# Taking the attention loop of a fused attention and two-layer kernel three steps at a time

## The chip, the cores and the metric

The kernel runs on one NeuronCore of a Trainium2 chip. The metric is device time of one execution in microseconds (us), lower is better. The kernel before took 828.43 us, the median of three runs (824.09 to 830.15). The profiled execution, from which every row below comes, took 831.28 us.

Engines: PE is TensorE (matrix products), DVE is VectorE, ACT is ScalarE, POOL is GpSimd, SP issues the DMAs. Each works through its own list of instructions in the order in which the program was written; semaphores hold an instruction back until what it needs is there.

## The reference, cut to what matters

```python
# q, k, v: 2 batches, 8 heads, 768 tokens, 64 wide; 16 cluster centroids a head
q_assign = argmax(q_n @ c_n.T);  k_assign = argmax(k_n @ c_n.T)
scores = where(q_assign == k_assign, (q @ k.T) / 8, -1e9)
scores = scores - max(scores, axis=-1)
attn = exp(scores);  attn = attn / (sum(attn, axis=-1) + 1e-9)
x = attn @ v                                  # then 1536 tokens x 512
x = f(x @ w_in) @ w_out                       # 512 -> 2048 -> 512; f(h) = h if h >= 1, 0 if h <= -1, else (h + 1)**2 / 4
x = rmsnorm(x);  out = (silu(x @ w_gate) * (x @ w_val)) @ w_out2
```

## The kernel before, in words

Attention goes over 8 **pairs** of heads (`NP`), and a pair over 12 **steps**: two halves of the queries (384 each) by six tiles of 128 keys. The global step number is `g`; pair p scores at g = 12p to 12p + 11. The program is written out by hand, without a scheduler, so what stands first in the code stands first on its engine.

For one step of a pair the kernel does the following.

- **Scores** (`score`, L348): for each of two heads two products of 128 x 384 on PE into one of three banks of PSUM (`st`), and an exponential on ACT (L357) into a tile P of 14. POOL adds the P tiles up (L363, L367), ten additions a half.
- **Values** (`values`, L369): P times v for both heads, each into one half of PE's columns (128 x 64 products). The two heads are side by side, and each product is recorded as two instructions.
- **Maxima** (`maxq`, L300): the row maxima, for the pair that scores later. Two products `mp` on PE into two banks (`mx`, two buffers), and a reduction of each on DVE (L319). A product needs the bank that the reduction two before it has read. After six steps of maxima, a small reduction (L322), a transposition on PE (`mt_ps`, L339), a copy on ACT (`mt`, L343) and a DMA bring the maxima into a row of A, where the scores' second product (L355) reads them.
- **Finish** (`finish`, L397), some steps after each half: piece 0 (ACT: logarithm, exponential, `r`), 1 and 2 (DVE: `e`, L413 and L416), 3 (DVE: `x`, L419), 4 (ACT: `xh`), 5 (DVE: `xl`, L423). The sums of P that it needs come from PE (`sums`, L391).
- **Preparation** (`prep`, L143) of a pair, about two pairs ahead: load q and k, split each into a high part (ACT) and a low part (DVE, L157), similarities with the centroids (PE, `simt`), a copy (ACT), transposition (PE, `sim`), the one-hot cluster (DVE: `mx` L187, `eq` L192, `e` L195, `m` L198, `oh` L202), transposition (PE, `oht_ps`), and the placing of the parts into A and B by DMA on SP's queue.

`attention_steps(g, n)` writes n steps: the maxima's copy of the previous group, the copy of finished values, then for each step its maxima, scores and other engines' work, then conversion of weights (`follow`, from g = 76), then the values of the **two steps before** (g - 2 and g - 1), sums, transpositions and similarities. From g = 0 on the kernel before calls it with n = 2. The small banks (`misc`, two buffers) serve the sums, the similarities and all transpositions by turns.

From g = 76 DVE and ACT also convert weights for the layers behind (`conv`, six DVE operations a slice, `conv(2)` a group and `conv(4)` from g = 84), and `TAIL` puts the first products of the layers between the last groups. The layers then run on PE without a pause to the end; the change does not touch them.

Of the kernel before, what the change touches and what calls it, by code (L numbers as in the profile page):

```python
# [12 lines left out]
ALU = mybir.AluOpType  # L13
# [23 lines left out]
def clustered_attention_two_ffn(  # L37
# [105 lines left out]
    def prep(p, o, on_tensor):  # L143
# [89 lines left out]
        def place(kind, s=slice(0, 2)):  # L233
# [19 lines left out]
            8: [lambda: sims_copy(), lambda: place("kh")],  # L253
            9: [lambda: place("qh")],
            10: [lambda: first_max()],
            11: [lambda: is_max(0), lambda: place("kl", 0)],
            12: [lambda: is_max(1), lambda: first_rank(), lambda: place("kl", 1)],
            13: [lambda: one_hot(), lambda: place("ql", 0)],
            14: [lambda: place("ql", 1)],
            17: [lambda: turn_out()],  # L260
# [32 lines left out]
        if p == 2:  # L293
            del todo[0]
            todo[-4] = [lambda: load_qk(p)]
        for f in (tensor if on_tensor else todo).get(o, ()):
            f()


    def maxq(p, j):  # L300
# [3 lines left out]
        if j == 0:  # L304
            st["M2", p] = ap.tile([128, 12, 2], F32, tag="M2", bufs=2, name=f"M2{p}")
            st["M", p] = ap.tile([128, 12], F32, tag="M", bufs=2, name=f"M{p}")
        if p == 0 and j < 8 and j % 3:

            mp = ps0.tile([128, 2, 512], F32, tag=f"mx{j % 3}", name=f"mp{p}_{j}")
            mp = [mp[:, 0], mp[:, 1]]  # L310
        else:
            mp = [ps.tile([128, 512], F32, tag="mx", bufs=2, name=f"mp{p}_{j}_{n}") for n in range(2)]
        for n in range(2):
            nc.tensor.matmul(mp[n][:, 0:HALF], A[0:112, h, 0, 128 * qt:128 * qt + 128],  # L314
                             Bk[0:112, h, 0, HALF * n:HALF * n + HALF], start=True, stop=True)
        if p == 0 and j < 10:
            warm(3 if j < 9 else 24, mp[1][:, HALF:512])
        for n in range(2):
# [490 lines left out]
    def preps(g, on_tensor=False):  # L809
        for p in range(NP):  # L810
            prep(p, g - PREP0[p], on_tensor)
# [186 lines left out]
```

## Time and profile before

| | before |
|---|---|
| median of three runs | 828.43 us |
| profiled execution | 831.28 us, of which the span from first to last instruction 829.5 us |
| PE busy | 806.4 us (97%) |
| DVE busy | 607.2 us (73%) |
| ACT busy | 350.2 us (42%) |
| POOL busy | 155.7 us (19%) |
| mean granted clock of TensorE | 0.985 |

Shares over the whole span say little here: attention takes roughly the first 260 us, and the layers the rest. Within attention there is a start of about 62 us, then pairs 1 to 5 (those that score at g = 12 to 71) at one even pace, then the seventh and eighth pair, where weights are converted as well. A busy PE is not a PE at its peak: an instruction that starts late because the array changes its layout looks busy all the same. So the start times of neighbouring PE instructions are read, not their busy time.

### The profile page before, as it was taken

Reading aid. Unit: us, or ns where it says so; the run is one execution under the profiler, and the core shown is the slowest. Engines: PE = TensorE matmul, PEld = TensorE weight load, DVE = VectorE, ACT = ScalarE, POOL = GpSimd, SP = SyncE. Lnnn points to the kernel's source line nnn. Section 1 sums busy time; section 2 is a strip of 40 time slices with the busy share of each in tenths; the row PEclk is TensorE's granted clock in tenths of the full one; section 3 lists DMA queues with packets and bytes.
Section 4 is the critical chain, followed back from the end, with each engine's and each line's share of the span. In section 5 each row is a group of like instructions: output and inputs, shape, how many; then the busy total and the mean of one; then the engine's idle time right before and its main releaser. Section 6 shows DMA issues by size and latency. Waiting matters only on the chain.

```text
span 829.5 us, 10698 instructions
## 1 busy us (share of the span) xinstructions
PE 806.4 (97%) x3817; PEld 611.7 (74%) x3817; DVE 607.2 (73%) x1101; ACT 350.2 (42%) x662; POOL 155.7 (19%) x163
## 2 busy tenths in 40 slices
PE   7789999999899999999999999999999999999998
PEld 3556665666455788888888888888888888888887
DVE  7658899988855788788777878898887875633333
ACT  5446666665435655553444353533333222211110
POOL 0368888888500000000000000000000000000000
PEclk9989999999899999999999999999999999999999
DMA  8956555653232537644443443145665343000003
GB/s 202 202 141 163 136 134 137 147 136 131 70 102 80 187 120 220 195 151 139 141 152 117 154 136 102 57 127 171 203 203 178 126 153 102 0 1 1 1 25 127
DMA packets 33336, 105.15 MB, mean 127 GB/s; under 512 B 5098, under 2 KB 5444, under 8 KB 33284
## 3 DMA queue, kind: packets, MB, share of 16 engines
q1 hardware_dynamic: 33284, 104.48, 42.5%
q8 instruction: 30, 0.49, 0.3%
q14 instruction: 22, 0.18, 0.1%
HBM read 81.02 MB, written 3.15 MB: 101 GB/s over the span
## 4 chain that ended last, share of the span: by engine, by line
PE 88%; DVE 8%; DMA 1%; ACT 1%; issue 0%; POOL 0%; ACTq 0%; POOLq 0%; DVEq 0%
PE h L545 40%; PE y L594 9%; PE y L593 9%; PE y L595 9%; PE pv L375 6%; PE mp L314 4%; DVE M L319 3%; PE sc L355 3%; PE sc L354 3%; PE sum L394 1%; DVE e L416 1%; PE sum L383 1%; DMA kraw<-kT 1%; PE simt L165 1%; DMA aa<-mt 1%; PE xt L663 1%
## 5 line engine op out<-in xcount | busy, mean ns | idle before, releaser
L367 POOL TENSOR_TENSOR acc<-acc,P 128x384 f32<-128x384 f32 x112 | 124.3, 1141 | 17.0 <-ACT P L357 17.0
L319 DVE TENSOR_REDUCE M<-mp 128x1 f32<-128x384 f32 x192 | 97.3, 549 | 35.1 <-PE mp L314 33.6
L357 ACT ACTIVATE P<-sc 128x384 f32<-128x384 f32 x192 | 84.5, 490 | 77.1 <-PE sc L355 68.2
L545 PE MATMUL h<-xh,bb 128*128 128x512 f32 x360 | 115.5, 390 | 0.0
L545 PE MATMUL h<-xh,aa 128*128 128x512 f32 x336 | 108.6, 391 | 0.0
L496 ACT ACTIVATE raw<-raw 128x512 f32<-128x512 f32 x60 | 40.7, 679 | 111.5 <-DVE bits L494 97.6
L545 PE MATMUL h<-xh,place 128*128 128x512 f32 x264 | 85.8, 392 | 0.0
L610 DVE TENSOR_TENSOR Y<-y,Y 128x512 f32<-128x512 f32 (+1 forms) x85 | 57.8, 681 | 31.9 <-PE y L595 31.8
L375 PE MATMUL pv<-P,v 128*64 128x384 f32 x384 | 80.2, 524 | 0.0
L545 PEld LDWEIGHTS h<-xh,bb 128*128 128x128 f32 x360 | 67.6, 188 | 14.7 <-issue 0.6
L545 PEld LDWEIGHTS h<-xh,aa 128*128 128x128 f32 x336 | 63.1, 188 | 15.0 <-issue 1.8
L355 PE MATMUL sc<-aa,bb 97*128 97x384 f32 x192 | 66.7, 348 | 3.6 <-DMA aa<-mt 3.6
L545 PE MATMUL h<-xl,bb 128*128 128x512 f32 x180 | 70.1, 390 | 0.0
L354 PE MATMUL sc<-aa,bb 112*128 112x384 f32 x192 | 67.0, 349 | 1.5 <-ACT P L357 1.5
L545 PE MATMUL h<-xl,aa 128*128 128x512 f32 x168 | 65.5, 390 | 0.0
L314 PE MATMUL mp<-bb,aa 112*128 112x384 f32 x192 | 59.7, 387 | 4.7 <-DVE M L319 4.6
L565 DVE SCALAR_TENSOR_TENSOR a<-h,a 128x512 f32<-128x512 f32 x48 | 33.1, 691 | 38.7 <-ACT a L561 38.7
L545 PEld LDWEIGHTS h<-xh,place 128*128 128x128 f32 x264 | 49.6, 188 | 11.1
L314 PEld LDWEIGHTS mp<-bb,aa 112*128 112x128 f32 x192 | 33.6, 196 | 30.7 <-DVE M L319 13.1
L545 PE MATMUL h<-xl,place 128*128 128x512 f32 x132 | 52.0, 394 | 0.0
L494 DVE SCALAR_TENSOR_TENSOR bits<-raw,bits 128x512 uint32<-128x512 uint32 x68 | 48.3, 711 | 1.5
L375 PEld LDWEIGHTS pv<-P,v 128*64 128x64 f32 x384 | 24.3, 142 | 31.4 <-issue 27.7
(188 smaller groups left out, 1546.5 us busy)
## 6 DMA issues: line engine op xcount, KB each, us to landing
raw<-w_out SPq DMA_DIRECT2D x28, 512.0 KB
mid<-w_out SPq DMA_DIRECT2D x28, 511.8 KB
raw<-w_in SPq DMA_DIRECT2D x16, 512.0 KB
mid<-w_in SPq DMA_DIRECT2D x16, 511.8 KB
raw<-w_gate SPq DMA_DIRECT2D x12, 512.0 KB
raw<-w_val SPq DMA_DIRECT2D x12, 512.0 KB
mid<-w_gate SPq DMA_DIRECT2D x12, 511.8 KB
mid<-w_val SPq DMA_DIRECT2D x12, 511.8 KB
```

The lines of the kernel that those rows point to most:

```text
L314: nc.tensor.matmul(mp[n][:, 0:HALF], A[0:112, h, 0, 128 * qt:128 * qt + 128], Bk[0:112, h, 0, HALF * n:HALF * n + HALF], start=True, stop= ...
L319: nc.vector.tensor_reduce(st["M2", p][:, j, n:n + 1], mp[n][:, 0:HALF], axis=AX.X, op=ALU.max)
L354: nc.tensor.matmul(sc, Bk[0:112, h, 0, ks], A[0:112, h, 0, qs], start=True, stop=False)
L355: nc.tensor.matmul(sc, Bk[0:97, h, 1, ks], A[0:97, h, 1, qs], start=False, stop=True)
L357: nc.scalar.activation(P, sc, AF.Exp, scale=0.125)
L367: nc.gpsimd.tensor_tensor(acc, acc, P, op=ALU.add)
L375: nc.tensor.matmul(pv[64 * h:64 * h + 64, 0:HALF], st["v", p][:, h, kt], st["P", p, i, h], start=(kt == 0), stop=(kt == NT - 1))
L545: nc.tensor.matmul(h, w[:, wi, fs], x[:, kc, cs], start=(n == 0), stop=(n == 11))
L593: nc.tensor.matmul(y[:, c], g[:, 0, fs], w[:, 0, c], start=(m == m0), stop=False)
L594: nc.tensor.matmul(y[:, c], g[:, 0, fs], w[:, 1, c], start=False, stop=False)
L595: nc.tensor.matmul(y[:, c], g[:, 1, fs], w[:, 0, c], start=False, stop=(m == ms[-1]))
L610: nc.vector.tensor_tensor(Y[:, c], y[:, c], Y[:, c], op=ALU.add)
```

## The change

From g = 12 to g = 83 (`TWOS = 84`), which are the second to the seventh pair, the loop takes three steps at a time instead of two. Within such a group PE's list goes one `mp`, one head's two score products, one `mp`, and so on, where before two `mp` stood together; all work of the other engines for the three steps comes after the scores of the group; and the values of **the same** three steps follow, where before they were those of the two steps before. At g = 10 the two-step loop takes two steps' values more, and the group at g = 84 therefore has none. The maxima run two `mp` products further ahead from g = 12.

The preparation is laid out for three-step groups: the split of k and q, the similarities and so on are moved by one to three steps, the copy of the similarities (`sims_copy`) to the start of a group, and one of the two placings `kl` ahead of the maxima's DMA on SP's queue. Finish pieces come one to three steps later. v is loaded three steps earlier. Conversion begins at g = 75 with `conv(3)` a group. The group that completes six maxima now always issues their transposition itself, which at the start puts the first pair's `mt_ps` ahead of the `mp` of its step 6.

```diff
-        for i, (nm, piece) in enumerate((("k", 0), ("k", 1), ("q", 0), ("q", 1))):
-            todo.setdefault(i + (3 if p > 2 else 7), []).insert(0, lambda nm=nm, piece=piece: split(nm, piece))
-        tensor = {7: [lambda: sims()], 9: [lambda: sims_back()], 15: [lambda: turn()]}
...
+            3: [lambda: split("k", 0)],
+            4: [lambda: split("k", 1), lambda: split("q", 0)],
+            6: [lambda: place("kh"), lambda: split("q", 1)],
+            7: [lambda: place("qh")],
+            8: [lambda: place("kl", 0)],
+            9: [lambda: first_max(), lambda: is_max(0), lambda: place("kl", 1)],
+            10: [lambda: is_max(1), lambda: place("ql", 0)],
+            11: [lambda: place("ql", 1)],
+            12: [lambda: first_rank(), lambda: one_hot()],
+            15: [lambda: turn_out()],
+        }
+        tensor = {5: [lambda: sims()], 6: [lambda: sims_back()], 12: [lambda: turn()]}
...
-        for piece, ds in enumerate(((7, 3), (8, 4), (9, 4), (10, 5), (11, 5), (12, 6))):
+        for piece, ds in enumerate(((7, 7, 3), (8, 9, 4), (9, 10, 4), (10, 11, 5), (11, 13, 5), (12, 15, 6))):
...
+        if n == 3:
+            for k in range(g, g + n):
+                preps(k, 2)
+        due = max(0, 2 * (max_to + 1 - MAX0) - at["max"])
         for k in range(g, g + n):
+            if n == 3:
+
+                for h in range(2):
+                    i = 2 * (k - g) + h
+                    maxima(due * (i + 1) // 6 - due * i // 6)
+                    scores_of(k, h)
+                continue
...
+        if n == 3:
+            for k in range(g, g + n):
+                other_engines(k)
         then()
+        while at["value"] <= min(to, END - 1):
+            vp, vi = divmod(at["value"], 12)
...
+            values(vp, vi)
...
-        conv(2 if g < 84 else 4)
+        conv(3 if g < 84 else 4)
...
-    for g in range(0, END + 6, 2):
+    steps = [(g, 2, g - 1 + 2 * (g == 10), g + 1) for g in range(0, 12, 2)]
+    steps += [(g, 3, g + 2, g + 3) for g in range(12, TWOS, 3)]
+    steps += [(g, 2, g - 1, g + 1) for g in range(TWOS, END + 6, 2)]
+    for g, n, to, max_to in steps:
...
-        if g == 74:
+        if g == 75:
             free += places[0:6]
```

PE's list before, at the end of the two-step group in which the third pair scores its steps 0 and 1. `mp` are the maxima of the same pair, `sc_1_0` the scores of step 1 and head 0, `P_10_0` those of step 10 of the pair before:

```order
L354 MATMUL sc_1_0_1090<-aa_109,bb_110 128x384
L355 MATMUL sc_1_0_1090<-aa_109,bb_110 128x384
L314 MATMUL mp_9_0_1097<-bb_110,aa_109 128x384
L314 MATMUL mp_9_1_1098<-bb_110,aa_109 128x384
L354 MATMUL sc_1_1_1103<-aa_109,bb_110 128x384
L355 MATMUL sc_1_1_1103<-aa_109,bb_110 128x384
L375 MATMUL pv_1_996<-P_10_0_1023,v_690 64x384
L375 MATMUL pv_1_996<-P_10_1_1029,v_690 64x384
L375 MATMUL pv_1_996<-P_11_0_1039,v_690 64x384
L375 MATMUL pv_1_996<-P_11_1_1051,v_690 64x384
```

PE's list of the change, at the end of the three-step group in which the same pair scores its steps 0 to 2:

```order
L328 MATMUL mp_11_0_1124<-bb_110,aa_109 128x384
L368 MATMUL sc_2_0_1127<-aa_109,bb_110 128x384
L369 MATMUL sc_2_0_1127<-aa_109,bb_110 128x384
L328 MATMUL mp_11_1_1133<-bb_110,aa_109 128x384
L368 MATMUL sc_2_1_1137<-aa_109,bb_110 128x384
L369 MATMUL sc_2_1_1137<-aa_109,bb_110 128x384
L387 MATMUL pv_0_1085<-P_0_0_1094,v_977 64x384
L387 MATMUL pv_0_1085<-P_0_1_1102,v_977 64x384
L387 MATMUL pv_0_1085<-P_1_0_1110,v_977 64x384
L387 MATMUL pv_0_1085<-P_1_1_1120,v_977 64x384
L387 MATMUL pv_0_1085<-P_2_0_1130,v_977 64x384
L387 MATMUL pv_0_1085<-P_2_1_1140,v_977 64x384
```

The `mp` stand apart, and the last values now read the P that the scores just above them feed.

DVE's list before, around the one-hot operations of a pair's preparation, with two reductions of maxima between every one or two other operations:

```order
L319 TENSOR_REDUCE M_1184<-mp_2_0_1238 128x1
L319 TENSOR_REDUCE M_1184<-mp_2_1_1239 128x1
L195 TENSOR_TENSOR e_1227<-eq_1226,rank 128x384
L198 TENSOR_REDUCE m_1258<-e_1227 128x24
L319 TENSOR_REDUCE M_1184<-mp_3_0_1273 128x1
L319 TENSOR_REDUCE M_1184<-mp_3_1_1274 128x1
L413 SCALAR_TENSOR_TENSOR e_1_1286<-sum_1_1233,r_1_1254 128x384
L202 TENSOR_TENSOR oh<-e_1227,m_1258 128x24x16
L319 TENSOR_REDUCE M_1184<-mp_4_0_1297 128x1
L319 TENSOR_REDUCE M_1184<-mp_4_1_1298 128x1
L416 SCALAR_TENSOR_TENSOR e_1_1286<-e_1_1286,r_1_1254 128x384
```

DVE's list of the change, from the end of a pair's second three-step group (scores of steps 3 to 5) into the third:

```order
L333 TENSOR_REDUCE M_1173<-mp_2_1_1211 128x1
L431 SCALAR_TENSOR_TENSOR e_0_1152<-e_0_1152,r_0_1143 128x384
L187 TENSOR_REDUCE mx_1230<-sim_1165 128x24
L192 TENSOR_TENSOR eq_1232<-sim_1165,mx_1230 128x384
L434 TENSOR_TENSOR x_0_1237<-pvs_0_908,e_0_1152 128x384
L195 TENSOR_TENSOR e_1233<-eq_1232,rank 128x384
L333 TENSOR_REDUCE M_1173<-mp_3_0_1256 128x1
L333 TENSOR_REDUCE M_1173<-mp_3_1_1264 128x1
L333 TENSOR_REDUCE M_1173<-mp_4_0_1272 128x1
L333 TENSOR_REDUCE M_1173<-mp_4_1_1282 128x1
L333 TENSOR_REDUCE M_1173<-mp_5_0_1292 128x1
L333 TENSOR_REDUCE M_1173<-mp_5_1_1301 128x1
```

Six reductions stand in a row, and five other operations in a row between two such sixes.

SP's list before and of the change, around the DMA that brings a pair's second six maxima (`mt_1`) into A:

```order
L68 DMA bb_108<-khl_994 64x1536 x2
L68 DMA aa_107<-qhl_1061 64x2x768 x2
L68 DMA aa_109<-mt_1_1180 1x3x128 x2
L68 DMA bb_108<-khl_994 32x768 x4
L129 DMA qraw_1262<-qT 128x768
```

```order
L68 DMA bb_108<-khl_1062 64x1536 x2
L68 DMA aa_107<-qhl_1067 64x2x768 x2
L68 DMA bb_108<-khl_1062 32x768 x2
L68 DMA aa_109<-mt_1_1169 1x3x128 x2
L68 DMA bb_108<-khl_1062 32x768 x2
```

Two placings of 32 x 768 now go ahead of the maxima.

## Rows read from the trace of the kernel before

**Rows 1.** Windows: length, then busy us (count) of PE, PEld, DVE, ACT, POOL; clock

```profile
114.38:140.47 26.09, 25.87 (x149) 16.48 (x147) 23.69 (x42) 16.89 (x39) 22.17 (x21) 1.00 0.60 144
192.71:223.82 31.11, 27.80 (x132) 16.53 (x131) 26.70 (x42) 15.23 (x35) 23.99 (x22) 0.90 0.36 121
```

**Rows 2.** Timeline of PE, one two-step group: start us, length us, instructions

```profile
99.89 0.81 PE L394 MATMUL sum<-acc,ones 128*64 128x384 f32 x4
100.53 0.81 PE L375 MATMUL pv<-P,v 128*64 128x384 f32 x4
101.28 0.62 PE L314 MATMUL mp<-bb,aa 112*128 112x384 f32 x2
101.73 0.34 PE L354 MATMUL sc<-aa,bb 112*128 112x384 f32 x1
...
103.32 0.34 PE L355 MATMUL sc<-aa,bb 97*128 97x384 f32 x1
103.59 1.51 PE L375 MATMUL pv<-P,v 128*64 128x384 f32 x8
105.03 0.62 PE L314 MATMUL mp<-bb,aa 112*128 112x384 f32 x2
```

**Rows 3.** Timeline of PE, two places where it is held up in that pair

```profile
106.65 0.91 PE L314 MATMUL mp<-bb,aa 112*128 112x384 f32 x2
...
109.56 0.27 PE L339 MATMUL mt_ps<-ident_f,M 128*6 128x128 f32 x1 [0.21 <-DVE M L322]
```

**Rows 4.** Chain that ended last, the stretch of a pair in which DVE carries it

```profile
127.87 1.02 DVE M L319 x2
...
135.67 0.27 PE mt_ps L339
```

**Rows 5.** DVE operations by form, 62 to 192.5 us: count, busy us, mean ns

```profile
L319 DVE TENSOR_REDUCE M<-mp 128x1 f32<-128x384 f32 x120 | 61.0, 548 | 13.6 <-PE mp L314 13.6
L419 DVE TENSOR_TENSOR x<-pvs,e 128x384 f32<-128x384 f32 x10 | 11.8, 1184 | 0.0
L416 DVE SCALAR_TENSOR_TENSOR e<-e,r 128x384 f32<-128x384 f32 x10 | 9.7, 971 | 0.0
L423 DVE SCALAR_TENSOR_TENSOR xl<-x,xh 128x384 fp32r<-128x384 f32 x10 | 9.5, 954 | 0.0
L157 DVE TENSOR_TENSOR qhl<-qraw,qhl 128x768 fp32r<-128x768 f32 x5 | 7.1, 1410 | 0.0
L413 DVE SCALAR_TENSOR_TENSOR e<-sum,r 128x384 f32<-128x384 f32 x10 | 5.5, 545 | 0.0
L202 DVE TENSOR_TENSOR oh<-e,m 128x384 bf16<-128x384 bf16 x5 | 4.8, 951 | 0.0
L157 DVE TENSOR_TENSOR khl<-kraw,khl 128x768 fp32r<-128x768 f32 x4 | 3.8, 942 | 0.0
```

**Rows 6.** Timeline of DVE: a first reduction of a group, and one operation at two lengths

```profile
101.76 1.02 DVE L319 TENSOR_REDUCE M<-mp 128x1 f32<-128x384 f32 x2 [1.01 <-PE mp L314]
125.83 0.55 DVE L423 SCALAR_TENSOR_TENSOR xl<-x,xh 128x384 fp32r<-128x384 f32 x1
139.37 1.37 DVE L423 SCALAR_TENSOR_TENSOR xl<-x,xh 128x384 fp32r<-128x384 f32 x1
```

**Rows 7.** Timeline of POOL over the first of those two operations

```profile
120.58 8.59 POOL L367 TENSOR_TENSOR acc<-acc,P 128x384 f32<-128x384 f32 x8 [0.79 <-ACT P L357]
```

**Rows 8.** Timeline of PE, seventh and eighth pair: two waits for DVE

```profile
218.06 1.15 PE L314 MATMUL mp<-bb,aa 112*128 112x384 f32 x2 [2.45 <-DVE M L319]
...
230.89 1.09 PE L314 MATMUL mp<-bb,aa 112*128 112x384 f32 x2 [1.30 <-DVE M L319]
```

**Rows 9.** Timeline of DVE, two operations of the weights' conversion

```profile
205.16 1.39 DVE L494 SCALAR_TENSOR_TENSOR bits<-raw,bits 128x512 uint32<-128x512 uint32 x1
...
208.95 0.42 DVE L498 TENSOR_SCALAR mid<-mid 128x512 uint32<-128x512 uint32 x1
```

**Rows 10.** Timeline of PE in the start: a wait for the maxima's DMA

```profile
47.48 0.69 PE L355 MATMUL sc<-aa,bb 97*128 97x384 f32 x1 [3.58 <-DMA aa<-mt]
```

More of the change, by code (lines that the diff above doesn't have):

```diff
@@ L141, in one_rows, with prep @@
                            ones[96:97].unsqueeze(1).to_broadcast([1, S // 64, 64]))
-    def prep(p, o, on_tensor):
+    def prep(p, o, which):
         A, Bk = AA[p % 3], BB[p % 3]
@@ L292, in prep, with maxq @@
             }
[L293 to L296, printed above, removed]
+        ahead = {6: [lambda: sims_copy()]} if p > 2 else {}
+        for f in (todo, tensor, ahead)[which].get(o, ()):
             f()
-    def maxq(p, j):
+    def maxq(p, j, n):
         A, Bk = AA[p % 3], BB[p % 3]
@@ L370, in values @@
         half, kt = divmod(i, NT)
-        if kt == 0:
-            st["pv", p] = banks["ps"].tile([128, 512], F32, tag="pv", name=f"pv{p}_{half}")
-        pv = st["pv", p]
+        pv = st["pv", p, half]
         for h in range(2):
@@ L387, in values_out, with values_bank @@
         x = ap.tile([128, HALF], F32, tag="fin", bufs=6, name=f"pvs{p}_{half}")
-        nc.scalar.copy(x, st["pv", p][:, 0:HALF])
+        nc.scalar.copy(x, st["pv", p, half][:, 0:HALF])
         st["pvs", p, half] = x
+    def values_bank(p, half):
+        st["pv", p, half] = banks["ps"].tile([128, 512], F32, tag="pv", name=f"pv{p}_{half}")
     def sums(p, half):
@@ L837, in scores_of, with sums_of @@
                 score(*divmod(g, 12), h)
-    def maxima_of(g):
-        for mp_, mj in max_at(g):
-            maxq(mp_, mj)
-    def values_of(g):
-        vp, vi = divmod(g - 2, 12)
-        if 0 <= vp < NP:
-            values(vp, vi)
+    def sums_of(g):
         sp, si = divmod(g - 5, 12)
@@ L849, in values_of, with maxima, attention_steps @@
             sums(sp, si // 6)
-    def attention_steps(g, n, then=lambda: None):
-        for rp, rj in max_at(g - 1):
-            if g >= 0 and rj in (5, 11):
-                max_rows(rp, rj // 6, 1)
-        for k in range(g, g + n):
-            vp, vi = divmod(k - 3, 12)
-            if 0 <= vp < NP and vi in (5, 11):
-                values_out(vp, vi // 6)
-        for k in range(g, g + n):
+    at = {"max": 0, "value": 0}
+    rows_due, rows_now, out_due = [], [], []
+    def maxima(n):
+        for _ in range(n):
+            p, j = divmod(at["max"] // 2, 12)
+            if p < NP:
+                maxq(p, j, at["max"] % 2)
+                if j in (5, 11) and at["max"] % 2:
+                    rows_due.append((p, j // 6))
+            at["max"] += 1
+    def attention_steps(g, n, to, max_to, then=lambda: None):
+        if g >= 0:
+            for r in rows_now:
+                max_rows(*r, 1)
+        del rows_now[:]
+        for p, half in out_due:
+            values_out(p, half)
+            if (p, half) != (NP - 1, 1):
+                values_bank(p + half, 1 - half)
+        del out_due[:]
+        if n == 3:
+            for k in range(g, g + n):
+                preps(k, 2)
+        due = max(0, 2 * (max_to + 1 - MAX0) - at["max"])
+        for k in range(g, g + n):
+            if n == 3:
[4 more added lines that the diff above has]
+                continue
             if k == g:
-                maxima_of(k)
+                maxima(due - due // 2 * (n - 1))
                 scores_of(k, 0, 1)
@@ L918, in clustered_attention_two_ffn @@
             cv["soon"] -= 6
-        attention_steps(g, 2, follow if g > 74 else lambda: None)
+        attention_steps(g, n, to, max_to, follow if g >= 75 else lambda: None)
         for _ in range(TAIL.get(g, 0)):
```

88 lines of the change are left out of this document (50 added, 38 removed).

## The prediction, made before the changed kernel was run

> **What bounds the kernel now.** I read the windows by stage first, since shares of the whole span mix attention with the layers. A pair takes 26.09 us [rows 1]; the five pairs that score from step 12 to step 71 agree within 0.01 us, so one pair stands for all. In it PE is recorded busy for 25.87 us, DVE for 23.69, POOL for 22.17 and ACT for 16.89. PE looks like the bound, with DVE close behind.
>
> Next the timeline of PE for one two-step group shows what "busy" hides [rows 2]. Inside the scores ten starts lie between 101.73 and 103.32 us, so a full-width product follows its neighbour after 1.59 / 9 = 0.177 us. The first score starts 0.45 after the group's first `mp`, where two products make 0.35: 0.10 is lost. The values start 0.27 after the last score: 0.09 is lost. Four half-width products take 0.64 (99.89 to 100.53), so eight take 1.28; the next group starts 1.44 after the first of them, and 0.16 is lost. Each change to half-width products and back so costs 0.35 us. A group of two steps is 3.75 us, which is 12 x 0.177 + 1.28 + 0.35 and nothing more.
>
> Then I looked for what holds PE up beyond that. In the stretch from 105 to 110 us a pair of `mp` takes 0.91 where 0.52 is usual and 0.62 opens a group, and a transposition waits 0.21 [rows 3]. That is about 0.6 us a pair. The chain of waits says why: from 127.87 to 135.67 us, once a pair, it runs over DVE [rows 4]. The lists shown above have the one-hot operations there, between the reductions.
>
> For 7.8 us a pair DVE is thus as tight as PE, and a gain on PE alone can run into DVE.
>
> **Fewer changes of layout.** Per 12 steps there are four groups where there were six. That removes 2 x 0.35 = 0.70 us of 26.09. The products are the same in number. If the 0.6 us of hold-ups vanish too, PE's floor is 26.09 - 0.70 - 0.6 = 24.8 us a pair.
>
> **Does DVE keep up?** A group of three steps is 18 x 0.177 + 1.92 + 0.35 = 5.45 us on PE, and 6.1 with the sums (0.64), which fall into the second and fourth group of a pair. What is left of the 24.8, some 1.7 us, are similarities and transpositions, in the other places.
>
> DVE's prices are the means by form less 0.08, since two reductions take 1.02 us and not 1.10 [rows 5, 6]: reduction 0.47, `x` 1.10, second `e` 0.89, `xl` 0.87, split of q 1.33, of k 0.86, first `e` 0.47, `oh` 0.87. `mx`, `eq`, `m` and the rank product are of the size of the first `e`, 0.47 to 0.5. A reduction starts 0.48 after its `mp` (101.28 to 101.76 us) [rows 2, 6], and in the new order one `mp` comes every 3 x 0.177 = 0.53. So six reductions end 0.48 + 5 x 0.53 + 0.47 = 3.6 us after a group's start, and DVE's other work follows in a block:
>
> - first group: 3.6 + small reduction 0.1 + q 1.33 + `e` 0.47 + `xl` 0.87 = 6.4. PE needs 5.45 + 0.45 of transpositions, and the next reduction could start 0.48 later: 6.4. It fits.
> - second group: 3.6 + `e` 0.89 + `mx` 0.47 + `eq` 0.47 + `x` 1.10 + rank 0.5 = 7.0, against 6.1 + 0.48 = 6.6. DVE is 0.4 late. PE's third `mp` of the third group needs the bank that the late reduction reads, so PE waits about 0.4.
> - third group: 3.6 + 0.1 + 0.47 + `oh` 0.87 + `e` 0.47 + `xl` 0.87 = 6.4, against 5.45 + 0.4 + 0.48: it fits. The transposition of the one-hot needs the small bank that `e` has read, which I put at 0.1 of waiting.
> - fourth group: 3.6 + 0.89 + 1.10 + 0.86 = 6.5, against over 7: it fits.
>
> So I expect 24.8 + 0.5 = 25.3 us a pair, 0.8 less than before, and 4.0 for five pairs. Bounds: no waiting at all gives 24.8. The other end lets every operation with two operands in SBUF take its long form: 1.37 was seen for `xl`, 0.55 for the same operation elsewhere [rows 6]. With `xl` and `e` at 1.3 and the splits at 1.33 the second group ends 0.8 to 1.0 late, the first and third 0.4, and the pair comes to about 26.5, 0.4 more than before.
>
> Here a rule speaks against the change. The row first: `xl` took 0.55 us at 125.83, inside a run of eight POOL additions from 120.58 to 129.17 us [rows 6, 7]; so meeting POOL does not always cost DVE an addition's length. The Trainium skill ("SBUF — State Buffer", Who interferes with whom) states that a DVE instruction with two SBUF inputs contends with a GpSimd instruction that reads SBUF, and that whichever starts first holds the shared ports for its whole length. By the rule alone each such operation would meet POOL, whose 22 us of work are 88% of a pair of 25.3, and the sum would be the upper end, 26.5; by the rows' means it is 25.3, and I keep the means.
>
> **Moved at nothing.** Values of the same steps need the last exponential of the group: the last P's products come 0.09 + 8 x 0.16 = 1.4 us after the last score, and ACT has a third of the pair free [rows 1]; if that cover fails, the price is one exponential a group, 4 x 0.5 a pair. The preparation's DMAs are the same in number; the maxima's DMA now follows two more placings on SP's queue but has three steps until its first reader where it had two. POOL's additions are the same and may lag by two groups before a P tile is missing.
>
> **Start and tail.** The start to step 11 is held by DMAs [rows 10] and keeps its order but for one transposition; I take 0. At step 10 the two steps' values move ahead: +1.3 us there, which the group at 84 does not have. Step 12 has two reductions more: +0.3.
>
> From the start of step 72 (192.71) to the last pair of `mp` (230.89) the kernel before takes 38.2 us; the first twelve steps of that are 31.11, 5 us over an even pair [rows 1, 8], because DVE also converts weights. PE waits 2.45 and 1.30 us for it [rows 8], and the `mp` behind these waits take 1.15 and 1.09 us where 0.62 is usual [rows 2]: the lower of the two clock levels (1.2 against 2.4 GHz). The window's granted clock is 0.90 [rows 1]. After the change the groups at 75, 78 and 81 convert three operations each, at 0.42 to 1.39 us [rows 9], say 0.95. DVE then needs 3.6 + 2.0 + 2.85 = 8.4 us against 6.1, so from there on DVE is the bound: 5.6 for the first group, about 8.1 for each of the next three (reductions back to back), 4.8 for the last two pairs of maxima with four conversions: 34.7. That leaves PE idle for about 1.8 us a group, between the 1.30 and 2.45 us after which the clock was low. If it falls in two groups, each stretches the reductions (four `mp` at 0.96 instead of 0.53: 1.7) and the tail is 38. I take the middle, 36.4: 1.8 less.
>
> **Sum** against the profiled execution of 831.28 us: -4.0 + 1.3 + 0.3 - 1.8 = -4.2, so 827.1 us. The three runs have their median 2.85 lower, at 828.43, so I forecast 828.43 - 4.2 = 824.2 us.
>
> **The rivals**, on the scale of the median.
>
> - *PE alone is the bound.* DVE's long operations fall where PE does not wait: 24.8 a pair (-6.5), tail 34.7 (-3.5), +1.3: 828.4 - 8.7 = 819.7 us. For it: DVE's work of 23.7 fits into 24.8. Against: the second group's sum, and 7.8 us a pair in which DVE already carries the chain [rows 4]. Chance 0.2.
> - *DVE takes the gain back*: 26.5 a pair, +2.0, tail unchanged, +1.6: 832.0 us. For it: POOL and DVE both get denser. Against: the means already hold such meetings. Chance 0.15. (The Trainium skill's rule on the shared ports, named above, would give this case.)
> - *Slower: the maxima's DMA comes late.* The second six maxima are copied at the start of a pair's second group and needed 6.1 us later, at the first score of the third. Two placings more stand ahead of it on SP's queue. In the start such a DMA held PE for 3.58 us and the product behind it took 0.69 where 0.34 is usual [rows 2, 10], so the clock fell as well. It decides from a landing later than 6.1 us after the copy. One wait of 1.5 us a pair and as much again at the low clock is 3 us, less the 0.8 gained: +11 for five pairs, 839 us. Against: no such wait in five even pairs, with a shorter time to land in. Chance 0.07.
> - *The forecast*: 824.2 us, chance 0.58, by itself 821 to 828.
>
> **How the numbers follow.** The forecast and the two neighbours hold 0.93; the range takes in most of the faster and the unchanged case, 817 to 832 us. About 1% (820.1 to 836.7) is what a measurement here can tell from no change. Faster by over 1%: half of the first rival and a little of the forecast's edge, 0.17. Slower by over 1%: the DMA and a little of DVE's case, 0.09. Within 1%: 0.74.
>
> **What would show it.** Pairs between 24.8 and 25.8 us in the windows; 5.45 us from the first `mp` of a group to the end of its values; a wait of some 0.4 us for the reduction at the third `mp` of a pair's third group, and hardly any in the first and fourth; the tail at 35 to 38 us. An even pair of 26 or more would refute the DVE sum; waits of values for exponentials would refute the cover I named; a wait for the DMA of `mt` would be the slower rival.

## The result, and the profile after

| | before | after |
|---|---|---|
| median | 825.88 us (9 runs, 823.33 to 831.22) | 833.92 us (9 runs, 832.38 to 837.29) |
| profiled execution | 831.28 us, span 829.5 | 833.92 us, span 831.9 |
| mean granted clock in it | 0.985 | 0.988 |

The changed kernel takes 1.008 times as long as the kernel before, with a 95% interval of 1.0054 to 1.0105. The forecast was 824.2 us, in a range of 817 to 832.

In every trace the layers behind the last values of attention take 558.4 to 558.5 us, so the whole difference lies in attention. Four landmarks of the two profiled executions divide it:

| stretch | before, us | after, us | difference |
|---|---|---|---|
| to the first `mp` of step 12 | 62.21 | 63.08 | +0.87 |
| steps 12 to 71, five pairs | 130.50 | 135.71 | +5.21 |
| step 72 to the last pair of `mp` | 38.18 | 36.63 | -1.55 |
| from there to the last values | 40.13 | 38.00 | -2.13 |

Of the five pairs the first takes 28.23 us, the next three 27.05 to 27.08, and the last, which has no preparation beside it, 26.27. Before, each took 26.09 to 26.11. So the pairs lost where they were to gain, and an even pair of 26 us or more is the sign by which the prediction called its sum for DVE refuted.

The windows of the kernel after: one even pair, the stretch from step 72 to the last `mp`, and from there to the last values (columns as in [rows 1]):

```profile
90.52:117.60 27.08, 25.70 (x150) 16.27 (x148) 26.34 (x43) 18.83 (x39) 23.20 (x21) 1.00 0.58 140
198.79:235.42 36.63, 30.34 (x151) 19.76 (x149) 31.00 (x52) 21.20 (x46) 22.57 (x22) 0.92 0.33 111
235.42:273.42 38.00, 37.05 (x178) 21.84 (x179) 21.45 (x42) 20.24 (x41) 0.00 (x0) 0.95 0.31 103
```

Beside [rows 1] PE's work in a pair is a little less (25.70 us for 25.87), and DVE's has grown from 23.69 to 26.34 us, although it executes the same operations. DVE is now busy for 97% of a pair, PE for 95%.

PE's timeline of the second group of that pair and the start of the third (start us, length us, instructions, in brackets the idle time ahead and what ended it):

```profile
97.80 0.42 PE L328 MATMUL mp<-bb,aa 112*128 112x384 f32 x1
...
98.94 0.37 PE L328 MATMUL mp<-bb,aa 112*128 112x384 f32 x1
...
103.20 0.81 PE L409 MATMUL sum<-acc,ones 128*64 128x384 f32 x4
103.95 0.44 PE L328 MATMUL mp<-bb,aa 112*128 112x384 f32 x1
...
106.50 0.45 PE L328 MATMUL mp<-bb,aa 112*128 112x384 f32 x1 [1.22 <-DVE M L333]
```

The group itself takes 6.15 us, as forecast (6.1). The third `mp` of the next group should start 1.14 us after that group's first, as 98.94 does after 97.80; it starts 2.55 after it. The wait of 1.22 us stands at the very place that the prediction named, with three times the size.

DVE's timeline over the same stretch, and POOL's additions under it, one at a time except in the last line, show why:

```profile
98.25 3.27 DVE L333 TENSOR_REDUCE M<-mp 128x1 f32<-128x384 f32 x6
101.44 1.22 DVE L431 SCALAR_TENSOR_TENSOR e<-e,r 128x384 f32<-128x384 f32 x1
102.58 0.55 DVE L187 TENSOR_REDUCE mx<-sim 128x24 f32<-128x384 f32 x1
103.16 0.56 DVE L192 TENSOR_TENSOR eq<-sim,mx 128x384 bf16<-128x384 f32 x1
103.64 1.26 DVE L434 TENSOR_TENSOR x<-pvs,e 128x384 f32<-128x384 f32 x1
104.82 1.15 DVE L195 TENSOR_TENSOR e<-eq,rank 128x384 bf16<-128x384 bf16 x1
105.90 3.26 DVE L333 TENSOR_REDUCE M<-mp 128x1 f32<-128x384 f32 x6
```

```profile
101.24 1.00 POOL L381 TENSOR_TENSOR acc<-acc,P 128x384 f32<-128x384 f32 x1
102.20 1.32 POOL L381 TENSOR_TENSOR acc<-acc,P 128x384 f32<-128x384 f32 x1
103.48 1.01 POOL L381 TENSOR_TENSOR acc<-acc,P 128x384 f32<-128x384 f32 x1
104.44 1.32 POOL L381 TENSOR_TENSOR acc<-acc,P 128x384 f32<-128x384 f32 x1
107.96 1.97 POOL L377 TENSOR_TENSOR acc<-P,P 128x384 f32<-128x384 f32 x2 [2.20 <-ACT P L371]
```

The reductions end where the sum had them: the next operation starts 3.64 us after the group's first `mp` (3.6 forecast). The block behind them takes 4.46 us instead of 3.43, and the next reduction starts 8.10 us after that `mp` instead of 7.0.

POOL adds during nearly the whole block. Three operations of the block read both inputs from SBUF, and each starts while an addition is under way. The second `e` ends 0.41 us after the addition that ends at 102.25, `x` 0.42 us after the one that ends at 104.49, and the rank product 0.21 us after the one that ends at 105.76. Alone they take 0.55, 0.55 and 0.35 us (next section): what lengthens them is the rest of the addition, less some 0.14 us. POOL then stands idle for 2.20 us while DVE reduces again, and the reductions, at 555 ns, are as long as without it.

DVE's operations by form from 63 to 198.8 us, to set beside [rows 5] (line, operation, count | busy us, mean ns):

```profile
L333 DVE TENSOR_REDUCE M<-mp 128x1 f32<-128x384 f32 x122 | 65.8, 555 | 6.2 <-PE mp L328 5.5
L434 DVE TENSOR_TENSOR x<-pvs,e 128x384 f32<-128x384 f32 x10 | 12.5, 1252 | 0.2
L431 DVE SCALAR_TENSOR_TENSOR e<-e,r 128x384 f32<-128x384 f32 x10 | 12.2, 1216 | 0.0
L438 DVE SCALAR_TENSOR_TENSOR xl<-x,xh 128x384 fp32r<-128x384 f32 x9 | 7.1, 790 | 0.0
L157 DVE TENSOR_TENSOR khl<-kraw,khl 128x768 fp32r<-128x768 f32 x4 | 7.0, 1755 | 0.0
L157 DVE TENSOR_TENSOR qhl<-qraw,qhl 128x768 fp32r<-128x768 f32 x5 | 6.8, 1354 | 0.5
L195 DVE TENSOR_TENSOR e<-eq,rank 128x384 bf16<-128x384 bf16 x5 | 5.8, 1153 | 0.0
L428 DVE SCALAR_TENSOR_TENSOR e<-sum,r 128x384 f32<-128x384 f32 x10 | 5.5, 551 | 0.5
```

The split of k went from 942 to 1755 ns, the second `e` from 971 to 1216, the rank product (583 before) to 1153. `xl` got shorter, 790 ns for 954, and so did `oh`, 557 for 951. The reductions and the first `e` hardly moved (548 and 545 before).

Waits of PE of 0.7 us and more between step 72 and the last `mp`, beside [rows 8]:

```profile
214.20 0.45 PE L328 MATMUL mp<-bb,aa 112*128 112x384 f32 x1 [1.59 <-DVE M L333]
222.25 0.44 PE L328 MATMUL mp<-bb,aa 112*128 112x384 f32 x1 [0.72 <-DVE M L333]
230.83 0.44 PE L368 MATMUL sc<-aa,bb 112*128 112x384 f32 x1 [1.82 <-ACT P L371]
233.03 0.69 PE L368 MATMUL sc<-aa,bb 112*128 112x384 f32 x1 [0.88 <-ACT P L371]
```

They are spread over more places and none is as long as 2.45 us. Two of them are for exponentials of ACT and not for DVE. In the start PE waits 4.00 us for the maxima's DMA where it waited 3.58 [rows 10].

### The profile page after: what moved, and what is told of

It reads as the page before. It is cut to its first block, busy times and chain, and to the rows that moved or that the text cites. A ratio compares the mean times of both kernels' runs of the same rounds, so it can differ in the third digit from the quotient of the medians.

```text
span 831.9 us, 10717 instructions
## 1 busy us (share of the span) xinstructions
PE 801.1 (96%) x3817; PEld 609.1 (73%) x3817; DVE 619.5 (74%) x1101; ACT 360.7 (43%) x662; POOL 158.9 (19%) x163
## 4 chain that ended last, share of the span: by engine, by line
PE 80%; DVE 15%; ACT 2%; DMA 1%; issue 1%; SPq 0%; DVEq 0%; POOL 0%; POOLq 0%; ACTq 0%
PE h L560 40%; PE y L609 9%; PE y L608 9%; PE y L610 9%; DVE M L333 6%; PE pv L387 3%; PE mp L328 3%; PE sc L369 2%; PE sc L368 2%; DVE e L431 2%; DVE x L434 1%; DVE khl L157 1%; PE sum L395 1%; DVE qhl L157 1%; DMA v<-vP 1%
## 5 line engine op out<-in xcount | busy, mean ns | idle before, releaser
L381 POOL TENSOR_TENSOR acc<-acc,P 128x384 f32<-128x384 f32 x112 | 129.6, 1188 | 12.0 <-ACT P L371 11.9
L333 DVE TENSOR_REDUCE M<-mp 128x1 f32<-128x384 f32 x192 | 101.8, 554 | 21.4 <-PE mp L328 19.7
L371 ACT ACTIVATE P<-sc 128x384 f32<-128x384 f32 x192 | 91.8, 492 | 56.8 <-PE sc L369 50.8
L328 PE MATMUL mp<-bb,aa 112*128 112x384 f32 x192 | 69.8, 383 | 10.9 <-DVE M L333 10.4
L387 PE MATMUL pv<-P,v 128*64 128x384 f32 x384 | 73.0, 508 | 0.9 <-DMA v<-vP 0.9
L328 PEld LDWEIGHTS mp<-bb,aa 112*128 112x128 f32 x192 | 36.2, 194 | 32.5 <-DVE M L333 16.6
```

The costliest lines, as they stand in the source:

```text
L328: nc.tensor.matmul(mp[:, i % len(ns), 0:HALF], A[0:112, h, 0, 128 * qt:128 * qt + 128], Bk[0:112, h, 0, HALF * i:HALF * i + HALF], start=T ...
L333: nc.vector.tensor_reduce(st["M2", p][:, j, i:i + 1], mp[:, i % len(ns), 0:HALF], axis=AX.X, op=ALU.max)
L371: nc.scalar.activation(P, sc, AF.Exp, scale=0.125)
L381: nc.gpsimd.tensor_tensor(acc, acc, P, op=ALU.add)
L387: nc.tensor.matmul(pv[64 * h:64 * h + 64, 0:HALF], st["v", p][:, h, kt], st["P", p, i, h], start=(kt == 0), stop=(kt == NT - 1))
```

## The experiments

Two theories stood at the outset. **Meeting POOL:** DVE's operations with two operands in SBUF become long because the new order puts them in a block that always falls on POOL's additions. **The block itself:** five operations in a row between two sixes of reductions are too much, wherever POOL is.

### Without most of POOL's additions

POOL adds only the first two P tiles of each half and head (2 of 10 additions remain), once in the kernel after and once in the kernel before:

```diff
-        elif kt > 1:
-            acc = st["acc", p, half, h]
-            nc.gpsimd.tensor_tensor(acc, acc, P, op=ALU.add)
```

> The changed kernel without POOL's additions of the third to sixth tile of each half (two of ten remain, so the sums of exponentials are incomplete; everything else is as in the changed kernel). Theory A: a pair takes 27.05 us because DVE's operations with two operands in SBUF, which now stand in blocks, each wait for a POOL addition (second e 1.22, x 1.25, split of k 1.75, rank product 1.15 us). Without additions these fall to about 0.55, 0.55, 0.95 and 0.6, the wait at the third product of maxima of a pair's third group (1.22 us) vanishes, and a pair takes 24.7 to 24.9 us. Theory B: the block of six reductions and its two banks hold PE back by themselves: a pair stays above 26.5 us and the wait stays near 1.2.

> The kernel before, with the same additions left out. Theory A: DVE's long operations (second e 1.39 or 0.55, x 1.18) become short here too, the hold-ups of 0.6 us a pair go, and a pair falls from 26.09 to about 25.5 us, so that three-step groups are then 0.7 us a pair ahead. Theory B: the kernel before hardly changes (26.0 or more).

The kernel after took 818.35 us and 25.28 to 25.31 a pair; the kernel before 820.48 us and 25.70. DVE by form, first the kernel after without these additions, then the kernel before without them:

```profile
L428 DVE SCALAR_TENSOR_TENSOR e<-e,r 128x384 f32<-128x384 f32 x10 | 5.5, 548 | 0.0
L431 DVE TENSOR_TENSOR x<-pvs,e 128x384 f32<-128x384 f32 x9 | 5.0, 552 | 0.1
L157 DVE TENSOR_TENSOR khl<-kraw,khl 128x768 fp32r<-128x768 f32 x4 | 3.8, 958 | 3.4 <-ACT khl L154 3.4
L195 DVE TENSOR_TENSOR e<-eq,rank 128x384 bf16<-128x384 bf16 x5 | 1.8, 351 | 0.0
```

```profile
L416 DVE TENSOR_TENSOR x<-pvs,e 128x384 f32<-128x384 f32 x10 | 5.5, 549 | 0.0
L413 DVE SCALAR_TENSOR_TENSOR e<-e,r 128x384 f32<-128x384 f32 x10 | 5.5, 545 | 0.0
```

With POOL quiet the same operations are short in both orders. POOL's additions therefore cost the kernel before 26.10 - 25.70 = 0.40 us a pair, and the kernel after 27.07 - 25.30 = 1.77. Without them three steps at a time are 0.40 us a pair ahead, instead of 0.97 behind. That is the loss in the pairs, shown from both sides. DVE is then busy for 21.89 us of a pair in the new order and 20.22 in the old, so part of the growth seen above is not POOL's: six reductions in a row follow PE's `mp` at 0.54 us, where two follow each other at 0.47.

### With six of the ten additions

The additions of the last two tiles of a half are left out:

```diff
-        elif kt > 1:
+        elif 1 < kt < 4:
```

> The changed kernel with six of POOL's ten additions a half (those of the fifth and sixth tile are left out, so the sums are incomplete). A dose between all ten (27.06 us a pair, 16.9 us over the floor for nothing else) and two (25.29). Theory A: between, 26.0 to 26.5 us a pair, with second e and x at 0.8 to 1.0 us. If DVE's lateness came from a few unlucky meetings, the pair would stay at 27 or fall all the way to 25.3.

It took 821.7 us, and a pair 25.28 to 25.30, no more than with two additions. The expectation of a value in between failed, and what it named as the other case, a fall all the way, came. The timelines of POOL and DVE in the second group of a pair say why:

```profile
96.07 1.99 POOL L381 TENSOR_TENSOR acc<-acc,P 128x384 f32<-128x384 f32 x2 [0.18 <-ACT P L371]
103.27 1.97 POOL L377 TENSOR_TENSOR acc<-P,P 128x384 f32<-128x384 f32 x2 [5.21 <-ACT P L371]
```

```profile
98.21 0.55 DVE L431 SCALAR_TENSOR_TENSOR e<-e,r 128x384 f32<-128x384 f32 x1
...
99.73 0.55 DVE L434 TENSOR_TENSOR x<-pvs,e 128x384 f32<-128x384 f32 x1
100.20 0.35 DVE L195 TENSOR_TENSOR e<-eq,rank 128x384 bf16<-128x384 bf16 x1
```

The block from 98.21 to 100.55 us lies wholly in POOL's idle time from 98.06 to 103.27. What counts is not how much POOL adds but whether it adds while the block runs. `xl` (791 ns) and the split of q (1357), which still start during additions, stayed long, and the pair lost nothing by it.

### Moving DVE's work

One operation of the block, the rank product, moved to the next group:

```diff
-            10: [lambda: is_max(1), lambda: place("ql", 0)],
+            10: [lambda: place("ql", 0)],
...
-            12: [lambda: first_rank(), lambda: one_hot()],
+            12: [lambda: is_max(1), lambda: first_rank(), lambda: one_hot()],
```

> The changed kernel with one DVE operation, the rank product, moved from a pair's second group to its third. Theory A: the second group's block is shorter by its 1.08 us, the wait in the third group falls from 1.22 to about 0.2, the third group's block grows and holds the fourth by up to 0.8: a pair falls from 27.05 to 26.2 to 26.5, 3 to 4 us in all, about 830 us. Theory B: the order among other operations does not matter and the pair stays at 27.

It took 834.99 us, 1.0091 times the kernel before (1.0064 to 1.0118), so it is no faster than the kernel after (1.008). The five pairs gained 1.2 us, but from step 72 to the last `mp` it took 38.51 us instead of 36.63, with a wait of 3.66 us for a reduction. A pair fell to 26.80 to 26.87 us, less than expected: the third group went from 7.49 to 7.23 us. PE's timeline at that group's end has a new wait for it:

```profile
110.94 0.51 PE L211 MATMUL oht_ps<-ident_b,oh 128*128 128x128 bf16 x6 [0.75 <-DVE e L428]
```

The transposition of the one-hot needs the small bank that the first `e` reads, and that now comes later. The prediction had put this wait at 0.1 us for the order without this move.

Then the whole block was broken up, with the other engines' work after each step of a group instead of after its last:

```diff
                     scores_of(k, h)
+                other_engines(k)
                 continue
...
-        if n == 3:
-            for k in range(g, g + n):
-                other_engines(k)
```

> The changed kernel with the other engines' work written after each step's scores, as in the kernel before, and not after the group's: DVE's operations stand between pairs of reductions again. If it is the standing in a block that makes each operation meet POOL, their mean lengths go back to those of before (second e 0.97, x 1.18, rank product 0.58) and a pair is shorter than 27.05; if the contention is only a matter of how busy POOL is, the lengths stay at 1.2 and, since PE then waits for DVE inside its scores, a pair is longer, 27.5 or more.

It took 845.24 us, 1.021 times the kernel before (1.0163 to 1.0256), and 29.27 to 29.30 a pair. The second `e` is short there (548 ns), but `x` takes 1346, `xl` 996 and the split of k 1762 ns, and PE waits for a reduction in three of four groups (0.54, 1.20 and 0.72 us). So the same work in pieces is worse here than in a block: with three steps of scores in a row the pieces delay banks that PE wants at once.

### Less work on DVE

The two `e` operations, which refine the reciprocal of the sums, are left out, and `x` is made with ACT's reciprocal `r0` directly (the **short finish**); the same in the kernel before:

```diff
-        elif piece == 1:
-            nc.vector.scalar_tensor_tensor(fin("e"), sm, 1e-9, st["r0", p], op0=ALU.add, op1=ALU.mult)
-        elif piece == 2:
...
-            nc.vector.scalar_tensor_tensor(e, e, 2.0, st["r0", p], op0=ALU.subtract, op1=ALU.mult)
...
-            nc.vector.tensor_tensor(fin("x"), st["pvs", p, half], st["e", p], op=ALU.mult)
+            nc.vector.tensor_tensor(fin("x"), st["pvs", p, half], st["r0", p], op=ALU.mult)
```

> The changed kernel with two DVE operations a half fewer, first and second e, the step that refines the reciprocal of the sums: x takes the reciprocal from ACT as it is (signs adapted; this drops the refinement). It takes 1.14 and 0.47 us from DVE's blocks and leaves POOL's additions. Theory A: the second group's block is 0.3 late and no more, the small bank is free sooner, a pair takes 25.5 to 25.8 us, 6 to 8 us in all, about 825 us. If POOL itself and not DVE were what the pairs wait for, a pair would stay above 26.7.

> The kernel before with the same two DVE operations dropped. Theory A: its pairs lose what DVE holds them up by, 26.10 to about 25.75 us, since 25.70 was the length without most additions; some 1.5 us in five pairs and 1 to 2 in the tail, about 823 us. With DVE relieved the three-step loop should then be level with or ahead of it in the pairs (25.6 against 25.75).

The kernel after took 822.82 us (0.9934 of the kernel before, 0.9908 to 0.996), the kernel before 820.12 us (0.9899, 0.9858 to 0.994). Windows of an even pair and of the stretch from step 72 to the last `mp`, first of the kernel after with the short finish, then of the kernel before with it:

```profile
87.53:112.69 25.16, 25.16 (x149) 16.24 (x147) 23.10 (x38) 18.64 (x39) 22.64 (x21) 1.00 0.62 151
188.15:224.83 36.68, 30.57 (x150) 20.24 (x148) 30.06 (x47) 20.90 (x46) 22.25 (x22) 0.91 0.33 110
```

```profile
90.26:115.53 25.27, 25.27 (x149) 16.50 (x148) 21.93 (x38) 16.92 (x38) 21.67 (x21) 1.00 0.60 146
187.59:221.39 33.80, 31.31 (x160) 19.44 (x159) 29.44 (x48) 20.16 (x46) 23.72 (x22) 1.00 0.35 117
```

PE is busy for the whole of both pairs, so this is the pair with PE alone as its bound: three steps are then 0.11 us ahead. POOL adds in full, and still the loss in the pair is gone: so PE does not wait for POOL itself, but for a block of DVE that ends later than PE's own work. From step 72 to the last `mp` three steps lose 2.9 us, at a clock of 0.91 against 1.00 and with a wait of 3.68 us for a reduction; to the last values 0.7 us of that are left (36.28 us behind the last `mp` against 38.43). By the medians the kernel after is 2.7 us behind here too.

### Where the `mp` stand

The kernel after with the short finish, but with the two `mp` of a step together:

```diff
-                    i = 2 * (k - g) + h
-                    maxima(due * (i + 1) // 6 - due * i // 6)
+                    i = k - g
+                    maxima((due * (i + 1) // 3 - due * i // 3) * (1 - h))
```

> The change with the short finish, and the two mp of each step together ahead of the step's scores, as the kernel before has them, instead of one ahead of each head's scores. If single mp cost PE time of their own (0.20 to 0.21 us to the next start where products in a row take 0.177), a group's scores take 3.35 instead of 3.42 us and the pair 24.85 to 24.95 instead of 25.15. If two mp together bring back the wait for a bank that a reduction still reads (0.1 us at each step), the pair is 25.15 to 25.5, no better.

It took 827.97 us and 26.41 to 26.44 a pair, outside both expectations. PE's timeline of one of its groups:

```profile
90.95 0.62 PE L328 MATMUL mp<-bb,aa 112*128 112x384 f32 x2
...
92.11 0.85 PE L328 MATMUL mp<-bb,aa 112*128 112x384 f32 x2
92.80 0.34 PE L368 MATMUL sc<-aa,bb 112*128 112x384 f32 x1
```

The second pair of each group takes 0.69 us to the next start instead of 0.35: its second product needs the bank that the group's second `mp` filled. In groups of three, to write one `mp` per head is thus worth 1.25 us a pair, a part of the change to which the prediction gave no price.

### The tail

Groups of three only in the five even pairs, and groups of two with `conv(2)` from step 72 on; first with the finish as it was, then with the short one:

```diff
-    TWOS = 84
+    TWOS = 72
...
-        conv(3 if g < 84 else 4)
+        conv(2 if g < 84 else 4)
...
-        if g == 75:
+        if g == 74:
```

> The change with groups of three steps only in pairs 1 to 5 (scores of steps 12 to 71); from step 72 on groups of two, values two steps behind and conv(2) a group, as before. If the five pairs cost what the change's profile showed, they stay at 27.05 to 27.10 us with the first at 28.2 (135.7 us in all, 5.2 more than before), and the end from the start of step 72 to the last mp returns to the 38.2 us of the kernel before, less at most the 1.3 us by which the values no longer lag when that stretch begins: about 1.5 us worse than the change, 834 to 836 us, ratio to before 1.008 to 1.012. If instead the rest of the loss in the medians came from the three-step tail (the change's median is 8.0 us above before's, of which the pairs explain 5.2), the time falls to about 830, ratio 1.005 or less.

> The same (groups of three only in pairs 1 to 5), with the short finish: the two e operations of DVE left out, x made with ACT's reciprocal. With the short finish groups of three took 25.15 us a pair and groups of two 25.27, but the tail was better with two. So both advantages together: last mp at 220.5 to 221 us against 221.4 with groups of two throughout, span 0.5 us or so shorter, 819 to 820 us, ratio 0.988 to 0.990. If the advantage of three steps in the pairs is lost where the loop returns to two, it is equal to the kernel before with the short finish (820.1, 0.990) or up to 1 us behind it.

With the old finish it took 833.81 us, 1.006 times the kernel before (1.0038 to 1.0081), with 135.64 us in five pairs, as in the kernel after, and 37.52 + 38.52 us from step 72 to the last values, where the kernel after took 36.63 + 38.00. So the three-step tail is not where the change lost. With the short finish it took 819.82 us, 0.9892 of the kernel before (0.9866 to 0.9917), last `mp` at 220.95. That is 1.1% less than the kernel before, and can't be told from groups of two throughout with the short finish (820.12).

### The kernel before once more

The medians differ by 8.0 us and the two profiled executions by 2.6 only. Executions of the kernel before spread from 822.6 to 832.7 us, those of the kernel after from 832.4 to 837.3. More traces of the kernel before were taken to see where it gains in its shorter executions.

> The kernel before, unchanged, profiled once more: its profiled execution took 831.28 us and lies high in the spread of its runs (822.6 to 831.4). Theory A: the five even pairs take 26.1 us here too, as their pace is set by the program, and what differs between executions lies in the start or in the tail, where the clock falls after waits. If instead the pace of the pairs varied from run to run, the comparison of the two pairs' lengths, 27.06 against 26.10, would not hold.

> The kernel before, unchanged, looked at a third time. Its two profiled executions (831.3 and 829.7 us, clock 0.983 to 0.985) lie above its median of 826 to 828. If its quicker executions (822 to 826 us, clock 0.989 to 0.996) differ from these only where the clock falls, a quick one shows the same 26.10 us a pair, and a tail from the start of step 72 to the last mp of 33 to 36 us instead of 38.2, without 1.15 us mp behind the waits. If the pairs themselves were quicker it would show 25.5 or less. Another execution of 829 to 831 us leaves it open.

> The kernel before, unchanged, a fourth look. Three profiled executions took 829.7 to 831.3 us, each with the same waits and the same stretches of the lower clock between 215 and 260 us, whose windows lack some 6.8 us of full clock. If the clock's falls in that stretch are what separates quick executions from long ones, an execution under 828 us shows the same 26.1 us a pair, the same waits of 2.45 and 1.30 us, and from the start of step 72 to the last values of attention 73 to 76 us instead of 78.3, with a clock of 0.9 or more in all its windows. If it is the start instead, the third pair begins earlier by what is gained and the 78.3 us stay. An execution of 829 us or more leaves it open.

> The kernel before, unchanged, a fifth look, expected as the fourth: under 828 us with 73 to 76 us from step 72 to the last values if the clock in that stretch makes the difference, 78.3 us and an earlier step 12 if the start does.

In the order of their numbers (e5, e12, e13, e14) they took 829.69, 830.08, 826.29 and 832.5 us. Three repeat the profile before: 26.1 us a pair and 78.0 to 78.4 us from step 72 to the last values. The one of 826.29 us has the same pairs too, but only 73.92 us there. Windows of the kernel before from step 72 to the last `mp` and from there to the last values, first in the execution of 831.28 us, then in that of 826.29:

```profile
192.71:230.89 38.18, 33.58 (x160) 20.79 (x159) 31.97 (x53) 20.03 (x46) 23.99 (x22) 0.91 0.31 102
230.89:271.02 40.13, 38.63 (x178) 22.23 (x180) 21.28 (x41) 19.36 (x40) 0.00 (x0) 0.91 0.31 102
```

```profile
192.10:227.46 35.36, 30.71 (x160) 19.46 (x158) 31.86 (x53) 20.05 (x46) 24.17 (x22) 1.00 0.32 111
227.46:266.02 38.56, 37.04 (x178) 21.54 (x179) 21.28 (x41) 19.35 (x40) 0.00 (x0) 0.96 0.31 105
```

PE's waits in the execution of 826.29 us are those of [rows 8], to 0.02 us:

```profile
217.46 0.91 PE L314 MATMUL mp<-bb,aa 112*128 112x384 f32 x2 [2.46 <-DVE M L319]
227.46 0.91 PE L314 MATMUL mp<-bb,aa 112*128 112x384 f32 x2 [1.32 <-DVE M L319]
```

In one execution the `mp` behind these waits take 1.15 and 1.09 us, in the other 0.91 and 0.91: behind the same wait the clock drops in one execution of the program and not in the next. The stretch is 4.4 us longer with the drops. The other executions fit this: of the executions of the kernel before whose clock is on record, those of 829.6 us or more had a mean granted clock of 0.983 to 0.987, and those under 825 us one of 0.991 to 0.996.

## Why the prediction was wrong

| term | forecast, us | measured, us |
|---|---|---|
| start, with step 10's values | +1.3 | +0.87 |
| step 12, two more reductions | +0.3 | +1.16 (first group 7.66, later ones 6.50) |
| five pairs beside that | -4.0 | +4.05 |
| step 72 to the last `mp` | -1.8 | -1.55 |
| last `mp` to the last values | 0 | -2.13 |
| around the span | 0 | +0.24 |
| sum against the profiled execution | -4.2 | +2.64 |
| from there to the median | -2.85 | 0 |

- **The step that failed is the price of DVE's block**: "by the rows' means it is 25.3, and I keep the means". In the second group the operations behind the reductions were put at 0.89 (second `e`), 0.47, 0.47, 1.10 (`x`) and 0.5 (rank product), and took 1.14, 0.58, 0.48, 1.18 and 1.08 to the next start. The block came 1.1 us later than forecast, and the wait was 1.22 instead of 0.4. The means of the kernel before belonged to its order, in which some of these operations started early in an addition of POOL and some at its end. In the first group the long split of k, at the end of the fourth, did the same: 6.50 us against 6.18 with six of the ten additions, where that split takes 0.96.
- **What decides is when an operation starts, not whether it overlaps POOL.** The split of k overlaps additions in the kernel before too, and takes 0.94 there (two additions and the split, from the trace before):

```profile
124.93 1.00 POOL L367 TENSOR_TENSOR acc<-acc,P 128x384 f32<-128x384 f32 x1
136.26 1.32 POOL L367 TENSOR_TENSOR acc<-acc,P 128x384 f32<-128x384 f32 x1
137.57 0.94 DVE L157 TENSOR_TENSOR khl<-kraw,khl 128x768 fp32r<-128x768 f32 x1
```

  It starts as the addition of 136.26 ends. The `xl` of 0.55 us at 125.83 [rows 6, 7] starts 0.10 us before the addition of 124.93 ends, and is free for the same reason; the prediction took from this row that a meeting does not always cost an addition's length, which is so, but what it costs is what is left of the addition. In the new order each split of k starts some 0.93 us before an addition ends and takes 1.75. `oh` and `xl` got shorter by the same rule: `oh` now starts 0.08 us before an addition ends, where it was 0.54, and `xl` 0.29 or 0.47 us before, where it had been 0.96 for every second one.
- **The rival that fits is "DVE takes the gain back"**, given 0.15. Its 26.5 us a pair were not an upper end: it left the rank product at 0.5 us and the split of k at 1.33. The argument against it, that the means already hold such meetings, was the error. The Trainium skill's rule ("SBUF — State Buffer", Who interferes with whom) was the better guide: by it operations with two inputs in SBUF contend with POOL, and those with at most one, outside the two-port modes, and reductions do not. The trace agrees: first `e`, which reads PSUM, 551 ns with POOL and 552 without, reductions 555, second `e` 1216 and 548.
- **The floor** of 24.8 us a pair was 0.3 to 0.5 too low: 25.16 with the short finish, where PE is busy throughout, 25.28 with POOL quiet. What the prediction took off was there. Summed from start to start on PE in an even pair with the short finish, groups of three against groups of two, two changes of layout fewer give 0.69 us, where 0.70 was forecast. The hold-ups that go with the short finish are 0.83 us (26.10 to 25.27), where 0.6 was. What it lacked is a price for `mp` that stand apart: behind the first product of a group the others start 0.185 us after each other in groups of three and 0.176 in groups of two. Over the 64 of a pair this is 0.58 us, which stood in the sum at nothing.
- **Step 12** stood at +0.3 for two reductions. Eight in a row lengthen two pairs of starts in the scores and delay what stands behind them: the transposition of the similarities waits 0.46 us for the first `e`. Together 1.16 us.
- **The tail** to the last `mp` came to the length forecast, 36.63 us for 36.4, but that was luck in part. The three groups that convert weights take 22.98 us, where 24.3 were forecast even without a fall of the clock. The last two pairs of `mp` take 8.09 where 4.8 were, with the waits of 1.82 and 0.88 us for ACT's exponentials, which the prediction did not have. The two misses cancel. And the tail was set against an execution with the lower clock there, where the kernel before also has executions without it (35.36 us). The carried shift of 2.85 us from profile to median is, as far as the one quick trace and the clocks of the others show, largely those other executions. So the lower clock was counted as a gain of the change and once more as part of the median.
- **Refuted**: values did not wait for exponentials in the pairs, and no DMA of maxima came late there. PE alone is the bound only when DVE has less to do.

What stays open: what delays the products where `mp` stand apart (the 0.58 us), what decides whether the clock drops behind a wait, and whether POOL's last additions could be moved under the reductions, in the 2.20 us in which it is idle. This wasn't tried.

## What to carry to other kernels

A mean duration holds for the order it was read in: where a change regroups operations, ask of each which neighbour on another engine it will meet and when in the neighbour's instruction it will start, and price it at its longest form until a row in the new arrangement says otherwise. Leaving a suspected neighbour's work out, in both kernels, gives the price of the meeting in one number. And where a profile holds stretches of low clock, set a forecast against an execution without them, or shift to the median, but not both.

## What the runs showed of the hardware

- A DVE operation with both inputs in SBUF that starts while one of POOL's 128 x 384 additions is under way waits for its end. In pairs 1 to 5 of both profiled executions, before and after, it ends 0.21 to 0.22 us behind that addition if it takes 0.35 us alone (the rank product), 0.41 to 0.42 if it takes 0.55 (second `e`, `x`, `xl`, `oh`), and 0.81 to 0.82 if it takes 0.95 (the splits). One that starts in the addition's last 0.14 us or so keeps its own length, as the split of k at 137.57 and `xl` at 125.83 do.
- An addition of POOL takes 0.99 to 1.0 us by itself, and 1.32 where it starts while such an operation of 0.55 us runs (102.20, 104.44). In the block of the second group DVE loses 2.2 us (4.53 from the start of the second `e` to the end of the rank product, 2.34 with six of the ten additions) and POOL's four additions some 0.6, so DVE bears most of it; spans on POOL are rough.
- The same waits of 2.46 and 1.32 us left the clock at 1.00 in one execution and were followed by 0.54 to 0.78 in windows of 5 us of others of the same program; the stretch from step 72 to the last values took 4.4 us less without the drops.
